# A two-layer transformer on one core: the first GELU rewritten with Tanh, and 63 softmax tiles given to VectorE

## The chip, the core and the metric

The kernel runs on one core of one Trainium2 chip. The metric is the device time in microseconds (us) of one execution, lower being better. A kernel's figure is the median of its timed runs, which were all taken in the fast state of the chip, unless said otherwise. PE is the tensor engine (PEld its weight loads), ACT the scalar engine, DVE the vector engine (VectorE), POOL GpSimd, SP the engine that starts most transfers.

## The reference, cut to what matters

Two layers, each an attention block and then a mixer with an MLP. S = 2048 rows, D = 448 columns, 16 heads of 28 columns, MLP width 1792, all in bf16.

```python
def _gelu(x):
    return jax.nn.gelu(x, approximate=True)

def _A_ref(x, wqkv, wo):                       # attention
    ...
    scores = jnp.einsum("bhqd,bhkd->bhqk", q, k) * (Dh ** -0.5)
    p = _softmax(scores, axis=-1)
    o = jnp.einsum("bhqk,bhkd->bhqd", p, v)
    ...
def _B_ref(x, w1, w2, w3, w4):                 # mixer and MLP
    h = _gelu(_layernorm(x, axis=-1) @ w1)     # the first GELU: 448 columns
    ...                                        # four groups of h shifted by -1, 1, -2, 2 rows
    x1 = x + hs                                # hs = shifted h @ w2
    h2 = _gelu(_layernorm(x1, axis=-1) @ w3) @ w4   # the second GELU: 1792 columns
    return x1 + h2

x = x + _A_ref(_layernorm(x, axis=-1), A_wqkv, A_wo)          # layer 0
x = x + _B_ref(_layernorm(x, axis=-1), B_w1, B_w2, B_w3, B_w4)
x = x + _A_ref(_layernorm(x, axis=-1), A_wqkv, A_wo)          # layer 1
x = x + _B_ref(_layernorm(x, axis=-1), B_w1, B_w2, B_w3, B_w4)
```

The softmax is the bulk of the element-wise work: 2 layers x 16 heads x 2048 x 2048 exponentials.

## The kernel before: the parts that matter here

**A fixed order per engine.** The kernel is written as Python generators. A list scheduler runs them once, when the kernel is built, with an assumed duration for every operation (the second argument of `op`) and a priority for every task, lower numbers first. What comes out is one fixed list of instructions for each engine. Each engine is given its list in that order, and semaphores hold an instruction back until its inputs are there. So the order comes from the assumed times, and the waits from the real ones: an engine whose next instruction isn't ready stands still, although a later one may be ready (PE does so at 610 us in the trace below).

**The exp stream.** `t_scores` makes bursts of three or two score tiles (128 keys x 512 queries each) in PSUM banks 0 to 2 or 3 and 4. One ACT instruction exponentiates the burst, 1536 or 1024 columns, into `PT`. `t_pv` then multiplies with the values. An exp waits for two things: its scores, and the PV matmuls that read its `PT` slots six bursts ago.

```python
def t_exp():
    for u, un in enumerate(units):               # un: the tiles of burst u
        yield ("wait", ("st", u))                # its scores
        if u >= 6:
            for (si, kb, j) in units[u - 6]:
                yield ("wait", ("pv", si, kb))   # PV of the burst whose PT slots it takes over
        ...
        yield op("act", 0.07 + n * w * 0.000833, lambda e, ...: e.activation(out=PT[:, s0:s0 + n, 0:w],
                 in_=ps[:, bk[0]:bk[0] + n, 0:w], func=ACT.Exp, scale=SCALE), ...)
```

**The mixers** run beside the exps of other rows. Their matmuls share PSUM banks 6 and 7 with the projections, and nearly all those banks are emptied by DVE. The GELUs are batched, because exp and `Gelu_apprx_tanh` don't share a table on ACT: the trace has a table load of 1283 ns before a batch and one before the next exp:

```python
# t_mixA, the first GELU: four groups of 112 features are evicted by DVE, then one GELU over all of them
ev = op("dve", c_ps(NW), lambda e, ...: e.tensor_copy(out=hT[0:112, grp, c0:c0 + NW], in_=ps[0:112, bi(b), 0:NW]), ...)
...
yield op("act", c_act(4 * NW), lambda e: e.activation(out=hT[0:112, :, c0:c0 + NW],
         in_=hT[0:112, :, c0:c0 + NW], func=ACT.Gelu_apprx_tanh), ..., tab="gelu")
```

**Fill matmuls.** `keep_pe_busy` puts matmuls without use (`wq_pad`, `ident`) where the plan sees PE idle, to keep its clock up. They go into free PSUM banks, and stand in PE's list like any other instruction.

**Dormant code.** A routine that exponentiates a score tile on DVE (`d_first`, `d_chain`) is there already, but `DVE_TILES` returns 0.

Of the kernel before, what the change touches and what calls it, by code (L numbers as in the profile page):

```python
# [7 lines left out]
ALU = mybir.AluOpType  # L8
# [448 lines left out]

def DVE_TILES(L, ch, g, p):
    return 0


PVB = 2
# [16 lines left out]
DPRIO = 3  # L479

def build_kernel(nc, A_x, A_wqkv, A_wo, B_x, B_w1, B_w2, B_w3, B_w4, out, n_layers=2):
# [13 lines left out]
    KSL = 6  # L495
# [4 lines left out]
    FS = 65536.0  # L500
    E0, E1, E2, E3 = 0.99992525, 0.69583285, 0.22606939, 0.07802301
# [43 lines left out]
    def n_dve(si):  # L545
        L, ch, g, p, kts, first, last = segs[si]
        if CHUNKS[L][ch][1] < 4:
            return 0
        return DVE_TILES(L, ch, g, len(kts))

    seg_kb = []
    seg_d = []
    stream = []
    dlist = []
    for si_, (L_, ch_, g_, p_, kts_, fi_, la_) in enumerate(segs):
        n_ = CHUNKS[L_][ch_][1]
        per = 4 // n_
        nd = n_dve(si_)
        kbs = [tuple(kts_[i:i + per]) for i in range(0, len(kts_), per)]
        dk = list(range(len(kbs) - nd, len(kbs)))  # L560
        seg_kb.append(kbs)
        seg_d.append(dk)
        for kb in range(len(kbs)):
            for j in range(4):
                if kb in dk:
                    dlist.append((si_, kb, j))
                else:
                    stream.append((si_, kb, j))
    units = []
    pos = 0  # L570
    while pos < len(stream):
        n_ = 3 if len(units) % 2 == 0 else 2
        units.append(stream[pos:pos + n_])
        pos += n_
    units_in = {}
    for u_, un_ in enumerate(units):
        units_in.setdefault(un_[-1][0], []).append(u_)
    slot_of = {}
    unit_of = {}
    for u_, un_ in enumerate(units):  # L580
        for k_, b_ in enumerate(un_):
            slot_of[b_] = 5 * ((u_ // 2) % 3) + (0 if u_ % 2 == 0 else 3) + k_
            unit_of[b_] = u_
# [4 lines left out]
    with st:  # L588
# [36 lines left out]
        kT = sb("kT", [128, 4, 512 * KSL], BF16)  # L625
        qT = sb("qT", [128, 4, 1024], BF16)
        vaug = sb("vaug", [128, 4 * KSL, 512], BF16)
# [14 lines left out]
        qd = sb("qd", [128, 512], FP32)  # L642
        ub = sb("ub", [128, 3, 512], FP32)
        rb = sb("rb", [128, 512], FP32)
# [18 lines left out]
        UB = ["u0", "u1", "u2"]  # L663
        xst = h2T[:, :, :].rearrange("p a b -> p (a b)").rearrange("p (t d) -> p t d", d=D)
# [28 lines left out]
        def vslot(L, t):  # L693
            return t if L == 0 else (t + 17 if t < 7 else t - 7)
# [418 lines left out]
        def t_fct(L, p, pp):  # L1113
            for g in range(4):
                yield ("wait", ("bc", L, p, g))
                yield ("wait", ("bc", L, pp, g))
            yield op("dve", 0.2, lambda e: e.tensor_tensor(out=dbc[:, L, p, :], in0=bcb[:, L, p, :], in1=bcb[:, L, pp, :], op=ALU.subtract),
                     reads=[("bcb", L, p, g) for g in range(4)] + [("bcb", L, pp, g) for g in range(4)], writes=[("dbc", L, p)])
            yield op("dve", 0.2, lambda e: e.tensor_scalar(out=db29[:, L, p, :], in0=dbc[:, L, p, :], scalar1=M29, scalar2=None, op0=ALU.mult),
                     reads=[("dbc", L, p), (("cols",), 1)], writes=[("db29", L, p)])  # L1120
            yield ("sig", ("db29", L, p))
            yield op("act", 0.25, lambda e: e.activation(out=fct[:, L, p, :], in_=dbc[:, L, p, :], func=ACT.Exp, scale=SCALE),
                     reads=[("dbc", L, p)], writes=[("fct", L, p)], tab="exp")
            yield ("sig", ("fct", L, p))

# [38 lines left out]
        def t_qp(si):  # L1164
            L, ch, g, p, kts, first, last = segs[si]
            yield ("wait", ("db29", L, p[1]))
# [3 lines left out]
                     reads=[qk, ("db29", L, p[1])], writes=[qk])  # L1170
            yield ("sig", ("qp", si))

        def unit_banks(u):
            return (0, 1, 2)[:len(units[u])] if u % 2 == 0 else (3, 4)[:len(units[u])]

# [11 lines left out]
        def d_chain(blk, ys, pd):  # L1187
            si, kb, j = blk
            w, s = num1(ys), slot_of[blk]
# [3 lines left out]
            q = qd[:, :]  # L1193
            pdt = PD[:, s, :]
            yield ("acq", ["q"])
            yield op("dve", c_ps(512), lambda e: e.scalar_tensor_tensor(out=q, in0=lo, scalar=E2 / E3 * FS, in1=lo, op0=ALU.add, op1=ALU.mult),
                     reads=[("yd", w)], writes=[("qd",)])
            yield op("dve", c_ps(512), lambda e: e.scalar_tensor_tensor(out=q, in0=q, scalar=E1 / E3 * FS * FS, in1=lo, op0=ALU.add, op1=ALU.mult),
                     reads=[("yd", w), ("qd",)], writes=[("qd",)])
            yield op("dve", 0.45, lambda e: e.tensor_scalar(out=pdt, in0=q, scalar1=E3 / FS ** 3, scalar2=E0, op0=ALU.mult, op1=ALU.add),  # L1200
                     reads=[("qd",)], writes=[("pd", s)])
            yield ("rel", "q")
# [3 lines left out]
            yield ("sig", ("db", si, kb, j))  # L1206

        def d_late(blk):
            pd = yield ("acq", PDS)
            slot_of[blk] = int(pd[2:])  # L1210
            ys = yield ("acq", YS)
            b = yield ("acq", MISC[0:2])
            yield from score_ops([blk], [bi(b)])
            late.discard(blk)
            yield ("spawn", d_first(blk, b, ys, pd), 1)

        late = set()

        def t_scores():
# [6 lines left out]
            pend = []  # L1226
            for u, un in enumerate(units):
# [5 lines left out]
                for blk in un:  # L1233
                    si = blk[0]
                    if si != cur:
                        for d_ in pend:
                            late.add(d_)
                            yield ("spawn", d_late(d_), 1)
                        cur = si
                        pend = [(si, kb, j) for kb in seg_d[si] for j in range(4)]  # L1240
                        total = len(pend)
                        yield ("sig", ("segstart", si))
                    yield from seg_ready(si, seg_kb[si][blk[1]])
                blks, banks = list(un), [b_ for b_ in unit_banks(u)]
                extra = []
                if pend and not late:
                    us = units_in[cur]
                    quota = -(-total * (us.index(u) + 1) // len(us))
                    for d_ in list(pend):
                        L = segs[cur][0]  # L1250
                        if len(blks) >= 4 or total - len(pend) >= quota:
                            break
                        if d_[2] in [b_[2] for b_ in blks] or any(("k", L, segs[cur][2], kc_of(L, kt)) not in SC.events for kt in seg_kb[cur][d_[1]]):
                            continue
# [3 lines left out]
                        slot_of[d_] = int(got[2][2:])  # L1258
                        pend.remove(d_)
                        blks.append(d_)  # L1260
                        banks.append(bi(got[0]))
                        extra.append((d_, got))
                yield from score_ops(blks, banks)
                for d_, got in extra:
                    yield ("spawn", d_first(d_, *got), 1)
                yield ("sig", ("st", u))
            for d_ in pend:
                yield ("spawn", d_late(d_), 1)

        def t_exp():  # L1270
            for u, un in enumerate(units):
                yield ("wait", ("st", u))
                if u >= 6:
                    for (si, kb, j) in units[u - 6]:
                        yield ("wait", ("pv", si, kb))
                bk = unit_banks(u)
                s0 = slot_of[un[0]]
# [7 lines left out]
                for (si, kb, j) in un:  # L1285
                    if j == 3:
                        yield ("sig", ("kb", si, kb))
# [5 lines left out]
        def t_pv():  # L1293
            yield ("wait", ("start",))
            yield ("acq", ["b5"])
            for si in range(len(segs)):
# [3 lines left out]
                todo = [kb for kb in range(len(kbs)) if kb not in seg_d[si]]  # L1300
                dtodo = list(seg_d[si])
# [4 lines left out]
                while todo or dtodo:  # L1306
                    if dtodo and (not todo or all(("db", si, dtodo[0], j) in SC.events for j in range(4))):
                        batch = [dtodo.pop(0)]
                        for j in range(4):
                            yield ("wait", ("db", si, batch[0], j))  # L1310
                        buf, key = PD, "pd"
                    else:
                        batch = todo[:PVB]
                        del todo[:PVB]
                        for kb in batch:
                            yield ("wait", ("kb", si, kb))
                        buf, key = PT, "pt"
                    for kb in batch:
                        for kt in kbs[kb]:
                            yield ("wait", ("v", L, kt))  # L1320
                    yield ("ready", [(key, slot_of[(si, kb, j)]) for kb in batch for j in range(4)] + ([("psw", 5)] if done == 0 else []))
                    for kb in batch:
                        for i, kt in enumerate(kbs[kb]):
                            vs = vslot(L, kt)
                            for j in range(4):
                                s = slot_of[(si, kb, j)]
# [4 lines left out]
                        if buf is PD:  # L1331
                            for j in range(4):
                                yield ("rel", "pd%d" % slot_of[(si, kb, j)])
# [21 lines left out]
        def t_norm(si):  # L1355
# [25 lines left out]
            if (L, ch) != (1, len(CHUNKS[1]) - 1):  # L1381
                yield ("acq", ["rT"])
# [5 lines left out]
                yield ("acq", ["rb"])  # L1388
# [395 lines left out]
```

## Time and profile before

| | before |
|---|---|
| median of 4 timed runs (range) | 1135.35 us (1133.80 to 1138.58) |
| ACT, PE, DVE, POOL busy in its first profile | 92, 94, 41, 22% |
| exp instructions, table loads | 819, 32 |

The first profile fell in the slow state: its first part and its clock row (tenths of full speed in 40 slices) are

```profile
span 1164.7 us, 34325 instructions
PE 1091.5 (94%) x15669; PEld 427.6 (37%) x15669; DVE 481.9 (41%) x946; ACT 1068.3 (92%) x922; POOL 258.0 (22%) x453
PEclk9888888888888888878888888888888888888888
```

The granted clock (the share of full speed at which PE was allowed to run) was 0.850 on the mean. For comparisons I use a second profile of the same kernel, run e1 below: 1130.14 us, clock 0.995. Its page, first part, chain of waits, and two groups of the costliest instructions (busy us, mean ns of one, then the engine's idle time before them and what ended it):

```profile
PE 1021.3 (91%) x15666; PEld 415.0 (37%) x15669; DVE 483.8 (43%) x946; ACT 1057.2 (94%) x922; POOL 257.7 (23%) x453
...
ACT 69%; PE 21%; DMA 3%; DVE 3%; POOL 1%; issue 1%; SPq 0%; ACTq 0%; POOLq 0%; DVEq 0%
...
L1280 ACT ACTIVATE PT<-ps 128x1536 bf16<-128x1536 f32 (+1 forms) x819 | 934.4, 1331 | 12.3 <-PE ps L1147 10.5
...
L1688 PE MATMUL ps<-wq_pad,ident 128*32 128x256 bf16 x3892 | 174.8, 275 | 3.2 <-DVE qT L1034 1.3
```

At full clock ACT is 69% of the chain that ended last. Its exps take 934 us and wait only 12 us in all. PE is 91% busy, but 175 us of that are fills. The table of stretches, from a second profile of the same kernel (columns: stretch, length, then busy us of PE, PEld, DVE, ACT and POOL, the clock, and the share and rate of DMA):

```profile
232.00:406.00 174.00, 158.00 (x2421) 63.07 (x2417) 60.94 (x104) 169.30 (x140) 35.32 (x60) 0.98 0.16 33
580.00:754.00 174.00, 159.72 (x2350) 64.88 (x2343) 80.37 (x175) 173.38 (x150) 29.15 (x59) 1.00 0.23 69
1080.00:1128.00 48.00, 43.37 (x826) 28.21 (x818) 17.88 (x35) 17.00 (x36) 9.49 (x21) 1.00 0.07 22
```

In the middle (232 to 928 us) ACT is busy for 97 to 99.6% of the time and DVE for 35 to 46%. In the last 48 us, nearly all of it the tail after the last exp (which ends at 1081.4 us), PE works and ACT is mostly idle. The kernel is bound by ACT and then by a tail of mixer work. These groups of ACT instructions, kept apart by shape (from a second profile of the same kernel; busy us, mean ns of one, then the engine's idle time before them and what ended it), are what the change goes for:

```profile
L1280 ACT ACTIVATE PT<-ps 128x1536 bf16<-128x1536 f32 x410 | 632.2, 1542 | 9.6 <-PE ps L1147 8.0
L1280 ACT ACTIVATE PT<-ps 128x1024 bf16<-128x1024 f32 x409 | 458.1, 1120 | 2.7 <-PE ps L1147 2.5
...
L1280 ACT ACT_TABLE_LOAD x15 | 19.2, 1283 | 0.3
L1526 ACT ACTIVATE hT<-hT 112x2048 bf16<-112x2048 bf16 x7 | 13.4, 1913 | 0.1
L1526 ACT ACT_TABLE_LOAD x8 | 10.3, 1283 | 0.1
```

### The profile page before, as it was taken

To read this page: it belongs to the slowest core of one execution; us is meant where nothing else is said; L and a number is where in the kernel's file an instruction comes from. 1 tells how busy PE (TensorE), PEld (TensorE's weight loads), DVE (VectorE), ACT (ScalarE), POOL (GpSimd) and SP (SyncE) were. 2 spreads that over 40 slices of the span, in tenths; PEclk is the share of its full clock that TensorE was granted. 3 is DMA by queue.
4 is the path that set the end of the run, shared out by engine and by line. 5 is a ranking of instruction groups with operands and counts; after the bars stand their busy time and mean duration, and the time that the engine had idled before them with its cause. 6 is when DMAs were issued, how large, how long until landed. Compare 5 with 4: busy or idle time off the path is not lost.

```text
span 1164.7 us, 34325 instructions
## 1 busy us (share of the span) xinstructions
PE 1091.5 (94%) x15669; PEld 427.6 (37%) x15669; DVE 481.9 (41%) x946; ACT 1068.3 (92%) x922; POOL 258.0 (22%) x453
## 2 busy tenths in 40 slices
PE   5999999999998989899999999999999999999898
PEld 2333333343333333223333433343333333344464
DVE  7763214422434334542466334513453523454332
ACT  5968999999999999989999999999999999999942
POOL 3221213302333013420243001102351300231121
PEclk9888888888888888878888888888888888888888
DMA  3483112003021022210311022313211110220100
GB/s 105 122 214 104 39 53 48 15 11 94 17 42 30 12 70 52 42 24 20 85 42 36 26 88 76 119 57 107 66 34 29 30 47 12 50 53 16 15 14 22
DMA packets 94666, 62.21 MB, mean 53 GB/s; under 512 B 64568, under 2 KB 84344, under 8 KB 94520
## 3 DMA queue, kind: packets, MB, share of 16 engines
q1 hardware_dynamic: 91256, 55.53, 18.3%
q0 software_dynamic: 2304, 3.67, 1.3%
q8 instruction: 123, 2.02, 0.8%
q10 hardware_dynamic: 960, 0.80, 0.2%
q14 instruction: 23, 0.19, 0.0%
HBM read 27.12 MB, written 15.71 MB: 37 GB/s over the span
## 4 chain that ended last, share of the span: by engine, by line
PE 49%; ACT 42%; DMA 4%; DVE 3%; POOL 1%; SPq 1%; issue 1%; ACTq 0%; DVEq 0%
ACT PT L1280 35%; PE ps L709 27%; PE ps L1147 12%; PE ps L700 10%; ACT h2T L1648 4%; DMA ub<-uscr 1%; ACT hT L1526 1%; ACT L1280 1%; ACT L1526 1%; ACT L1648 1%; DMA rT<-ub 1%; DVE xn L853 1%; PE ps L1688 1%; DMA xT<-xn 1%; DMA PT<-in_A_wqkv_dram 0%
## 5 line engine op out<-in xcount | busy, mean ns | idle before, releaser
L1280 ACT ACTIVATE PT<-ps 128x1536 bf16<-128x1536 f32 (+1 forms) x819 | 945.5, 1285 | 32.9 <-PE ps L1147 29.5
L1147 PE MATMUL ps<-qT,kT 32*128 32x512 bf16 (+1 forms) x2304 | 325.6, 367 | 28.7 <-ACT PT L1280 21.3
L700 PE MATMUL ps<-PT,vaug 128*32 128x512 bf16 (+1 forms) x2304 | 271.0, 381 | 0.2 <-DVE ub L1371 0.2
L1147 PEld LDWEIGHTS ps<-qT,kT 32*128 32x128 bf16 x2304 | 80.0, 91 | 343.6 <-ACT PT L1280 224.0
L1688 PE MATMUL ps<-wq_pad,ident 128*32 128x256 bf16 x3892 | 191.0, 292 | 2.3 <-DVE qT L1034 1.3
L709 PE MATMUL ps<-xT,w 128*32 128x512 bf16 (+1 forms) x2240 | 188.2, 388 | 3.4 <-DMA xT<-xn 2.2
L709 PE MATMUL ps<-w,h2T 128*32 128x448 bf16 x1624 | 121.3, 389 | 13.1 <-ACT h2T L1648 13.1
L1688 PEld LDWEIGHTS ps<-wq_pad,ident 128*32 128x32 bf16 x3892 | 112.9, 100 | 43.0 <-issue 18.1
L1639 DVE CAST h2T<-ps 128x512 bf16<-128x512 f32 (+2 forms) x112 | 67.7, 605 | 118.7 <-PE ps L709 110.5
L700 PEld LDWEIGHTS ps<-PT,vaug 128*32 128x32 bf16 x2304 | 71.5, 95 | 101.1 <-issue 86.8
L1393 POOL TENSOR_TENSOR otn<-ub,rb 128x512 bf16<-128x512 f32 (+1 forms) x32 | 38.6, 1206 | 289.4 <-DMA rb<-rscr 283.5
L709 PEld LDWEIGHTS ps<-xT,w 128*32 128x32 bf16 x2240 | 62.4, 98 | 63.6 <-issue 34.1
L709 PEld LDWEIGHTS ps<-w,h2T 128*32 128x32 bf16 x1624 | 44.9, 101 | 56.1 <-issue 17.7
L961 POOL TENSOR_TENSOR sq<-kT 128x512 bf16<-128x512 bf16 (+2 forms) x32 | 30.1, 941 | 118.5 <-DVE kT L975 118.4
L709 PE MATMUL ps<-xT,wk_pad 128*32 128x512 bf16 (+2 forms) x576 | 49.9, 392 | 0.9 <-DVE xT L876 0.6
L961 POOL TENSOR_TENSOR sq<-qT 128x512 bf16<-128x512 bf16 x28 | 29.3, 1048 | 95.3 <-DVE qT L1008 85.9
L709 PE MATMUL ps<-xT,wq_pad 128*32 128x512 bf16 x512 | 47.7, 417 | 0.7 <-DVE vaug L1050 0.5
L1371 DVE SCALAR_TENSOR_TENSOR ub<-ub,fct,ps 128x512 f32<-128x512 f32 x24 | 17.9, 747 | 69.6 <-PE ps L700 67.2
L1384 DVE RECIPROCAL rT<-rT 16x128 f32<-16x128 f32 (+1 forms) x32 | 30.0, 936 | 38.4 <-DMA rT<-ub 38.4
L709 PE MATMUL ps<-wv,xT 128*32 128x448 bf16 x512 | 43.6, 381 | 1.1 <-DVE vaug L1050 0.8
L1660 DVE TENSOR_TENSOR x_res<-x_res,ps 128x448 f32<-128x448 f32 x16 | 9.9, 621 | 83.1 <-PE ps L709 83.1
L709 PE MATMUL ps<-wo_pad,otn 128*32 128x448 bf16 x512 | 42.2, 384 | 2.1 <-DVE x_res L1444 2.1
(133 smaller groups left out, 892.9 us busy)
## 6 DMA issues: line engine op xcount, KB each, us to landing
rb<-rscr SPq DMA_DIRECT2D x28, 256.0 KB
uscr<-ub SPq DMA_DIRECT2D x24, 256.0 KB
ub<-uscr SPq DMA_DIRECT2D x24, 256.0 KB
xnd<-xn SPq DMA_DIRECT2D x28, 128.0 KB, 1.8
x_res<-in_A_x_dram POOLq DMA_DIRECT2D x16, 224.0 KB, 2.9
xd<-x_res SPq DMA_DIRECT2D x16, 224.0 KB, 1.9
x_res<-xd SPq DMA_DIRECT2D x16, 224.0 KB
out_dram<-obf SPq DMA_DIRECT2D x16, 112.0 KB
```

The source lines that it names most:

```text
L700: return lambda e: e.matmul(out=out, lhsT=lhsT, rhs=rhs, start=start, stop=stop, **kw)
L709: r.append(e.matmul(out=out[c:c + w, :], lhsT=lhsT[:, c:c + w], rhs=rhs, start=start, stop=stop, tile_position=(0, c)))
L961: return op("pool", 0.15 + NW * 0.0018, lambda e: e.tensor_tensor(out=sq[:, si, 0:NW], in0=src, in1=src, op=ALU.mult), reads=rk, writes=[( ...
L1147: yield op("pe", max(0.055, 0.22 / nc_ * NW / 512.0), lambda e, i=i, kc=kc, j=j, g=g, a=a, NW=NW, bank=bank: e.matmul(out=ps[:, bank, i * ...
L1280: yield op("act", 0.07 + n * w * 0.000833, lambda e, bk=bk, s0=s0, n=n, w=w: e.activation(out=PT[:, s0:s0 + n, 0:w], in_=ps[:, bk[0]:bk[0] ...
L1371: yield op("dve", c_ps(NW), lambda e: e.scalar_tensor_tensor(out=u, in0=u, scalar=fct[:, L, p[1], g:g + 1], in1=ps[:, 5, 0:NW], op0=ALU.mu ...
L1384: yield op("dve", 0.75, lambda e: e.reciprocal(out=rT[0:4 * n, :], in_=rT[0:4 * n, :]), reads=[("rT",)], writes=[("rT",)])
L1393: yield op("pool", 0.2 + NW * 0.0021, lambda e: e.tensor_tensor(out=otn[:, g, 0:NW], in0=u, in1=rb[:, 0:NW], op=ALU.mult), reads=[uk, ("rb ...
L1526: yield op("act", c_act(4 * NW), lambda e: e.activation(out=hT[0:112, :, c0:c0 + NW], in_=hT[0:112, :, c0:c0 + NW], func=ACT.Gelu_apprx_tanh),
L1639: ev = op("dve", c_ps(NW), lambda e, fch=fch, b=b: e.tensor_copy(out=hb[:, fch, 0:NW], in_=ps[:, bi(b), 0:NW]), reads=[("ps", bi(b))], wri ...
L1648: yield op("act", c_act(nl * NW), lambda e: e.activation(out=h2T[:, 0:nl, 0:NW], in_=h2T[:, 0:nl, 0:NW], func=ACT.Gelu_apprx_tanh), reads= ...
L1688: return [e.matmul(out=ps[32 * c:32 * c + 32, bi(b), 0:256], lhsT=ident[:, 32 * c:32 * c + 32], rhs=wq_pad[:, 0, 0:256], start=True, stop= ...
```

## The change

The intent is to take work from ACT, the bound, and give it to DVE, which is idle more than half of the time.

1. **Tanh GELU.** The first GELU is written out with Tanh, which needs no table change beside exp: DVE evicts z = 0.5x, POOL squares, DVE, ACT Tanh, DVE. Eight batched GELUs become 32 short Tanh, and 16 table loads go.
2. **Tiles on DVE.** In chunks 0 to 3 of layer 0 and 0 to 2 of layer 1, some 6% of a segment's score tiles (3% in one chunk), 63 in all, are taken as an extra head of a score burst. A tile goes to bank 6 or 7, if a bank, a `yd` and a `PD` buffer are free in the plan. Five DVE operations make the exp. The chain of the last four has priority 5, behind nearly everything else.
3. **Plumbing.** Bursts are put together on the fly; three shared `fb` buffers serve the chain, the Tanh and the normalization; there is one KV slot less; bias differences are made per group of heads; a few more normalizations go through PE.

```diff
+DPRIO = 5
+DLO = 4
+DHI = 8
+def DRATE(L,ch,g): return {(0,0):.06,(0,1):.06,(0,2):.06,(0,3):.03,(1,0):.06,(1,1):.06,(1,2):.06}.get((L,ch),0)
 ...
 # t_scores
+                    for kb in range(kb0 + DLO, min(kb0 + DHI, nkb)):
+                        ...
+                        got = yield ("try", [MISC[0:2], YS, PDS])
+                        if got is None:
+                            break
+                        blk = (si, kb, js[0])
+                        home[blk] = ("pd", int(got[2][2:]))
 ...
 # d_chain, after d_first (yd <- scaled scores) has emptied the bank
-            yield ("acq", ["q"])
+            fr = yield ("acq", FB, [("yd", w)])
             yield op("dve", c_ps(512), ... q = (lo + c) * lo ...)
             yield op("dve", c_ps(512), ... q = (q + c) * lo ...)
-            yield op("dve", 0.45, lambda e: e.tensor_scalar(out=pdt, in0=q, ...))
+            yield op(DTS[0], DTS[1], lambda e: e.tensor_scalar(out=pdt, in0=q, ...))
             yield op("dve", c_ps(512), ... PD = hi * 128 + PD, as int16 ...)
 ...
 # t_mixA
-                    ev = op("dve", c_ps(NW), ... tensor_copy ...)
+                    ev = op("dve", c_ps(NW), ... tensor_scalar, times 0.5 ...)
+                    yield ("spawn", t_tanh(L, t0, grp, hT[0:112, grp, c0:c0 + NW], NW, hk), pr)
-                yield op("act", ... Gelu_apprx_tanh over the four groups ...)
+        def t_tanh(L, t0, grp, z, NW, hk):
+            yield op("pool", 0.2 + NW * 0.0021, ... f = z * z ...)
+            yield op("dve", 0.1 + NW * 0.00108, ... f = (f + 0.25 / GK) * z ...)
+            yield op("act", c_act(NW), ... f = Tanh(scale * f) ..., tab="exp")
+            yield op("dve", 0.1 + NW * 0.00108, ... z = (f + 1) * z ...)
```

Counted in the built programs: exps 819 to 794, table loads 32 to 16, DVE instructions 946 to 1355, fill matmuls 3892 to 3092.

## The prediction

> **What bounds it now.** The page's first part: ACT busy 1068 of 1165 us (92%), PE 1092 (94%), DVE 482 (41%), POOL 258 (22%). In the stretches table ACT is 54 to 58 us busy in nearly every 58 us between 116 and 1102 us. PE's 94% is inflated: 3892 fill matmuls (line 1688) run 191 us, most between 58 and 232 and between 754 and 928 us; in 406 to 580 and 928 to 1102 they take only 16 to 17 of 174 us, so there PE is nearly full too. The chain of waits agrees: PE 49%, ACT 42%. From 1112 us on (after the last exp) it is PE alone, about 52 us. So: ACT bounds the light stretches, ACT and PE together the mixer stretches, PE the tail.
>
> **What ACT loses** (instruction counts from the two built programs):
> - 63 score tiles leave: 794 exp instructions for 819. A pair of 1536 and 1024 columns costs 2.27 us in the timeline (48 in 54.41 us), so about 0.43 us a tile plus 25 fixed parts: 28 us.
> - The mixer's first GELU (8 batches, 14.4 us) becomes 32 Tanh (28 of 512, 4 of 256 columns), about 15 us: no gain by itself. But table loads go from 32 to 16. The Trainium skill (ScalarE: Activation LUTs, "Table sets: the hidden batching unit") puts tanh in exp's set; the built program has no load before a Tanh. A load is 1.283 us in this trace: 20 us.
> Together about 47 us of ACT.
>
> **What it adds.** DVE: five operations for each of 63 tiles, estimated 0.5 to 0.75 us each from like operations (TENSOR_SCALAR from PSUM 0.745, SCALAR_TENSOR_TENSOR 0.747): about 210 us; two more per Tanh: about 43 us. DVE goes to about 720 us, some 65%. Where POOL runs too, one TENSOR_SCALAR from SBUF took 965 ns instead of 499, so more is possible. POOL gains 32 squares, about 32 us. The fourth head rides in a score burst: 25 fewer bursts on PE; fills drop from 3892 to 3092. The three layer-1 g=3 normalizations and one more go through PE instead of DMAs: small.
>
> **How much is critical.** The tiles lie in chunks 0 to 3 of layer 0 and 0 to 2 of layer 1, over half where PE still runs fills, so most of the saving there counts. At the end it does not: in the new program six 512-column GELU tiles of the chunk before last, and its second half of work, come after the last exp; before they came ahead of it. The tail grows by an estimated 12 to 18 us of PE work. I expect about 30 of 47 us.
>
> **Time:** 1105 us, 8 in 10 between 1084 and 1128. Chances: faster by over 2% 0.70, within 2% 0.27, slower 0.03.
>
> **What the profile will show if right.**
> 1. ACT busy about 1020 us, with 16 table loads and 794 exps.
> 2. DVE about 720 us, chain operations 0.5 to 0.8 us each.
> 3. Stretch 58 to 232 us of before shortened most; ACT's share of the middle stays above 94%.
> 4. Time from last exp to end grows from 52 to about 65 us.
> 5. Fill time on PE down by about 40 us; PE's share of the chain up.
> 6. Waits of scores for ACT fall; no large wait of PE on DVE `PD`.
>
> **What would make it wrong.** DVE in order: five-operation chains delay PSUM evictions, PE waits for banks 6 and 7 and the scores stall (then waits of PE on DVE grow by tens of us, near 1125). DVE operations slowed by POOL beyond 1 us each. The other way, PE may have more slack in the unprofiled runs (1135 against 1165 us profiled, where the granted clock is 0.85) and the whole 47 us appear: about 1088.

## The result, and the profile after

| | before | after |
|---|---|---|
| median of 4 timed runs (range) | 1135.35 us (1133.80 to 1138.58) | 1120.95 us (1118.73 to 1121.54) |
| mean granted clock of 32 fast runs of before, 4 of after | 0.990 | 0.976 |

The ratio is 0.9866, with a 95% interval of 0.9840 to 0.9891. Every ratio here is the mean time of one kernel's fast runs over that of the other's in the same rounds, so it is not quite the ratio of the medians. The change won 14 us where I had expected 30. The time lies in the range; "faster by over 2%", the likeliest class, did not happen.

The page after, with the lines that answer to those of before:

```profile
PE 1009.0 (90%) x14936; PEld 405.6 (36%) x14939; DVE 721.7 (65%) x1355; ACT 1010.1 (90%) x910; POOL 305.9 (27%) x481
...
ACT 58%; PE 26%; DVE 10%; DMA 3%; POOL 2%; issue 1%; SPq 0%; ACTq 0%; DVEq 0%
...
L1286 ACT ACTIVATE PT<-ps 128x1536 bf16<-128x1536 f32 (+1 forms) x794 | 912.0, 1323 | 52.6 <-PE ps L686 28.6
...
L1699 PE MATMUL ps<-wq_pad,ident 128*32 128x256 bf16 x3092 | 140.9, 278 | 5.7 <-DVE x1b L1597 3.1
```

ACT's busy time fell by 1057.2 - 1010.1 = 47.1 us. But the idle time before exps went from 12.3 to 52.6 us, and DVE's share of the chain from 3 to 10%. The stretches of the middle show it too; ACT is no longer busy nearly all the time, and DVE's work in the first one has doubled. The last line is the tail:

```profile
232.00:406.00 174.00, 156.57 (x2296) 59.24 (x2294) 122.98 (x208) 163.79 (x138) 45.91 (x66) 0.97 0.15 34
580.00:754.00 174.00, 157.76 (x2317) 62.99 (x2316) 103.75 (x220) 164.61 (x145) 28.06 (x40) 0.98 0.21 67
1055.00:1117.00 62.00, 56.71 (x1074) 35.13 (x1066) 20.13 (x39) 23.46 (x42) 9.34 (x21) 1.00 0.06 19
```

ACT's groups after: 32 Tanh with no table load at their line, and 7 loads at the exps instead of 15.

```profile
L1540 ACT ACTIVATE fb<-fb 112x512 f32<-112x512 f32 x28 | 18.6, 669 | 0.0
...
L1286 ACT ACT_TABLE_LOAD x7 | 9.0, 1283 | 0.1
...
L1540 ACT ACTIVATE fb<-fb 112x256 f32<-112x256 f32 x4 | 2.7, 670 | 0.0
```

The Trainium skill says that tanh is in exp's table set (ScalarE: Activation LUTs, "Table sets: the hidden batching unit"); the trace agrees, with 16 loads left for the second GELU and the start. The chain's five operations on DVE:

```profile
L1201 DVE SCALAR_TENSOR_TENSOR PD<-yd,PD 128x512 int16<-128x512 int16 x63 | 49.2, 788 | 0.7
L1196 DVE SCALAR_TENSOR_TENSOR fb<-fb,yd 128x512 f32<-128x512 f32 x63 | 44.7, 719 | 0.5
L1194 DVE SCALAR_TENSOR_TENSOR fb<-yd 128x512 f32<-128x512 uint16 x63 | 43.9, 710 | 0.4
L1180 DVE TENSOR_SCALAR yd<-ps 128x512 int32<-128x512 f32 x63 | 43.1, 686 | 48.0 <-PE ps L1139 47.6
L1198 DVE TENSOR_SCALAR PD<-fb 128x512 bf16<-128x512 f32 x63 | 33.0, 532 | 0.4
```

The work of a tile is 0.69 + 0.71 + 0.72 + 0.53 + 0.79 = 3.43 us. But from the start of the first to the end of the last operation a tile took 7.7 us on the median and 24.3 at most.

**Where the time went.** Here is an account of both profiles (e1 for before), one execution each. "Idle" is the sum of all gaps of ACT that end between 60 us and the end of the last exp. The differences were taken before rounding.

| us | before (e1) | after | difference |
|---|---|---|---|
| start to first exp | 25.4 | 24.3 | -1.2 |
| ACT's idle | 22.2 | 52.0 | +29.8 |
| the rest up to the last exp, mostly ACT work | 1033.7 | 980.1 | -53.6 |
| tail after the last exp | 47.0 | 60.6 | +13.5 |
| span | 1128.4 | 1116.9 | -11.5 |

The work ahead of the last exp fell by more than 47 us because the last large batch of the second GELU moved behind the last exp: ACT works 22.1 us in the tail of after, 15.6 in that of before, 6.5 more. (No table load moved with it; there is one in the tail before and after.) So up to the last exp 53.6 + 1.2 = 54.8 us went, and 29.8 us of new idle time came back; the tail took 13.5 more.

The waits of ACT (what waited for what, total us, times, longest) name the new idle time. Before, then after:

```profile
ACT PT L1280 <- PE ps L1147: 10.5, 12, 2.7
ACT fct L1122 <- DVE dbc L1117: 10.2, 2, 7.1
```

```profile
ACT PT L1286 <- PE ps L686: 28.6, 12, 4.5
ACT PT L1286 <- PE ps L1139: 22.2, 26, 4.2
```

Before, exps waited 10.5 us, for scores only (L1147), and never for PV. After, they waited 28.6 us for PV (L686), which is new, and 22.2 us for scores (L1139). The 10.2 us for `fct`, a wait for bias differences, went with the plumbing; run e4 below, which has the plumbing alone, doesn't show it either.

The longest of the new gaps can be followed. ACT's timeline (start, length, instruction, idle before and its releaser), and the chain that ended last, in order of time:

```profile
611.75 1.45 ACT L1286 ACTIVATE PT<-ps 128x1536 bf16<-128x1536 f32 x1 [4.49 <-PE ps L686]
```

```profile
603.26 1.07 DVE xn L839 x2
604.33 0.60 DVE x1b L1597
...
607.13 1.32 DVE xn L839
608.45 0.54 DVE st L824
...
609.11 0.39 DVE PD L1198
609.51 0.60 DVE x1b L1597
...
610.13 0.63 DVE st L824
610.76 0.83 DVE xn L839
...
611.68 0.58 DVE PD L1201
...
612.31 0.34 PE ps L686
```

For nine microseconds the chain runs through DVE alone, apart from two short POOL operations that are cut out here. Mixer work (`xn`, `x1b`, `st`) and a tile's chain (`PD`) take turns there. PE's timeline shows two ways in which DVE's delay stops PE:

```profile
610.15 0.95 PE L1699 MATMUL ps<-wq_pad,ident 128*32 128x256 bf16 x28 [1.25 <-DVE x1b L1597]
...
612.31 0.39 PE L686 MATMUL ps<-PD,vaug 128*32 128x512 bf16 x1 [0.42 <-DVE PD L1201]
```

First, PE's next instruction is a fill into a bank that DVE hasn't emptied yet (`x1b`), and the PV behind it in PE's list, at 611.34, releases the exp. A fill is not free here: after the wait, PE works through 28 of them for 0.95 us ahead of that PV. Then a PV waits for the tile itself. Over the whole run these two kinds of instruction waited for the chain's last operation (us in total, times):

```profile
  PEld ps L686: 11.1, 12
  PE ps L686: 6.5, 7
```

A weight load and its matmul often wait for the same thing, so the two must not be added: PE's matmuls lost 6.5 us this way. Of the 12 waits of exps for PV, two (3.2 and 2.3 us) follow such a wait. Most of the others follow evictions on DVE, as above, or come while PE runs at half clock (see e11). All waits of PE's matmuls for DVE between 60 us and the last exp grew from 8.8 us before to 20.3.

### The profile page after: what moved, and what is told of

It is laid out like the page before. It is cut to its first block, busy times and chain, and to the rows that moved or that the text cites. A ratio compares the mean times of both kernels' runs of the same rounds, so it can differ in the third digit from the quotient of the medians.

```text
span 1116.9 us, 33256 instructions
## 1 busy us (share of the span) xinstructions
PE 1009.0 (90%) x14936; PEld 405.6 (36%) x14939; DVE 721.7 (65%) x1355; ACT 1010.1 (90%) x910; POOL 305.9 (27%) x481
## 4 chain that ended last, share of the span: by engine, by line
ACT 58%; PE 26%; DVE 10%; DMA 3%; POOL 2%; issue 1%; SPq 0%; ACTq 0%; DVEq 0%
ACT PT L1286 52%; PE ps L695 14%; PE ps L1139 6%; PE ps L686 5%; ACT h2T L1659 4%; DVE xn L839 2%; DMA ub<-uscr 1%; ACT fb L1540 1%; ACT L1659 1%; DVE qT L994 1%; DVE PD L1201 1%; DVE x1b L1597 1%; DVE PD L1198 1%; DVE st L824 1%; PE ps L1699 1%
## 5 line engine op out<-in xcount | busy, mean ns | idle before, releaser
L1286 ACT ACTIVATE PT<-ps 128x1536 bf16<-128x1536 f32 (+1 forms) x794 | 912.0, 1323 | 52.6 <-PE ps L686 28.6
L1139 PE MATMUL ps<-qT,kT 32*128 32x512 bf16 (+1 forms) x2304 | 315.4, 365 | 47.6 <-ACT PT L1286 37.6
L686 PE MATMUL ps<-PT,vaug 128*32 128x512 bf16 (+1 forms) x2241 | 246.9, 366 | 1.9 <-DVE ub L1367 1.1
L1139 PEld LDWEIGHTS ps<-qT,kT 32*128 32x128 bf16 x2304 | 78.2, 91 | 328.5 <-ACT PT L1286 286.1
L695 PE MATMUL ps<-xT,w 128*32 128x512 bf16 (+2 forms) x2240 | 169.0, 364 | 4.8 <-DMA xT<-xn 1.9
L1699 PE MATMUL ps<-wq_pad,ident 128*32 128x256 bf16 x3092 | 140.9, 278 | 5.7 <-DVE x1b L1597 3.1
L686 PEld LDWEIGHTS ps<-PT,vaug 128*32 128x32 bf16 x2241 | 68.0, 95 | 92.7 <-issue 76.0
L1699 PEld LDWEIGHTS ps<-wq_pad,ident 128*32 128x32 bf16 x3092 | 85.6, 97 | 36.4 <-issue 14.6
L1391 POOL TENSOR_TENSOR otn<-ub,fb 128x512 bf16<-128x512 f32 (+1 forms) x28 | 36.2, 1293 | 166.2 <-DMA fb<-rscr 159.0
L1180 DVE TENSOR_SCALAR yd<-ps 128x512 int32<-128x512 f32 x63 | 43.1, 686 | 48.0 <-PE ps L1139 47.6
L1538 POOL TENSOR_TENSOR fb<-hT 112x512 f32<-112x512 bf16 (+1 forms) x32 | 36.3, 1136 | 69.3 <-DVE hT L1520 66.3
L1201 DVE SCALAR_TENSOR_TENSOR PD<-yd,PD 128x512 int16<-128x512 int16 x63 | 49.2, 788 | 0.7
L1196 DVE SCALAR_TENSOR_TENSOR fb<-fb,yd 128x512 f32<-128x512 f32 x63 | 44.7, 719 | 0.5
L1194 DVE SCALAR_TENSOR_TENSOR fb<-yd 128x512 f32<-128x512 uint16 x63 | 43.9, 710 | 0.4
```

Source lines behind the costliest of these rows:

```text
L686: return lambda e: e.matmul(out=out, lhsT=lhsT, rhs=rhs, start=start, stop=stop, **kw)
L695: r.append(e.matmul(out=out[c:c + w, :], lhsT=lhsT[:, c:c + w], rhs=rhs, start=start, stop=stop, tile_position=(0, c)))
L1139: yield op("pe", max(0.055, 0.22 / nc_ * NW / 512.0), lambda e, i=i, kc=kc, j=j, g=g, a=a, NW=NW, bank=bank: e.matmul(out=ps[:, bank, i * ...
L1180: yield op("dve", c_ps(512), lambda e: e.tensor_scalar(out=y, in0=ps[:, bi(bank), :], scalar1=SCALE * L2E * FS, scalar2=-126.0 * FS, op0=A ...
L1194: yield op("dve", c_ps(512), lambda e: e.scalar_tensor_tensor(out=q, in0=lo, scalar=E2 / E3 * FS, in1=lo, op0=ALU.add, op1=ALU.mult), read ...
L1196: yield op("dve", c_ps(512), lambda e: e.scalar_tensor_tensor(out=q, in0=q, scalar=E1 / E3 * FS * FS, in1=lo, op0=ALU.add, op1=ALU.mult), ...
```

## The experiments

Each run's edit is against the kernel after, except for e1. All gave correct results. The times are medians of four timed runs (six for e12) with their ranges.

### e1: before, looked at once more

No edit: the kernel before, one look, to have its profile at full clock.

> The kernel before once more, for a profile in the fast state: the one at hand was taken at a granted clock of 0.85 and took 1165 us, the changed kernel's at 0.977, so the two cannot be set side by side. All theories: about 1134 us, ACT busy again 1068 us (its clock is not what was throttled). Theory DVE-delay (the chains on VectorE arrive late, PE waits for them in program order and the exponentials wait for PE): the fast profile of before shows under 15 us of ACT gaps over 0.7 us in the middle, against about 42 us in the changed kernel's. Rival tail theory (the saving is real in the middle and lost after the last exp): ACT gaps in the middle about alike in both, and the time after the last exp longer by 12 us or more in the changed kernel (61 us there).

It took 1130.14 us at clock 0.995. ACT was busy 1057 us and not 1068. Its gaps over 0.7 us add up to 17.2 us, somewhat over the 15 expected (10.2 of them are the waits for `fct`), against 43.6 in after; and the tail is 13.5 us shorter than after's. So there is something in both theories. Its profile is the one used above. The PE half of the chain in the first profile (PE 49%, ACT 42%) was the slow state's: here it is ACT 69%, PE 21%.

### e2, e3, e4: one part alone, and neither

```diff
# e2: no tiles, Tanh kept
-def DRATE(L,ch,g): return {(0,0):.06,(0,1):.06,(0,2):.06,(0,3):.03,(1,0):.06,(1,1):.06,(1,2):.06}.get((L,ch),0)
+def DRATE(L,ch,g): return 0
# e3: the batched GELU back, tiles kept
-   ev = op("dve", ... tensor_scalar, times 0.5 ...);  t_tanh(...) for each group
+   ev = op("dve", ... tensor_copy ...);  one op("act", ... Gelu_apprx_tanh ...) for the four groups
# e4: both edits, so that only the plumbing is left
```

> The changed kernel without its tiles on VectorE (rate 0; all else kept: 16 table loads, 819 exps, 0 tiles). DVE-delay theory: the Tanh alone keeps its 20 us of table loads and the tiles gave about nothing, so this is 1113 to 1123 us, equal to the changed kernel within 0.5%. Tail theory: the tiles' 28 us are lost only in part; this is 1128 us or more.

> The changed kernel with the batched GELU of before, tiles kept (34 loads, 793 exps, 65 tiles). DVE-delay theory: tiles alone give little, 1128 to 1138 us. Tail theory, and any in which the tiles' saving counts: 1112 to 1125 us.

> The changed kernel with neither tiles nor Tanh: what is left is the plumbing (one key slot fewer, normalization of some groups through PE, bias differences by group). All theories: 1130 to 1140 us, as before. If it is faster than before by over 0.5%, a part of the gain is the plumbing's.

| run | time (range) | ratio to before (95%) | idle of ACT | tail |
|---|---|---|---|---|
| e2, Tanh alone | 1122.68 (1114.19 to 1126.85) | 0.9887 (0.9836 to 0.9939) | 28.6 | 61.4 |
| e3, tiles alone | 1115.99 (1113.73 to 1116.86) | 0.9833 (0.9799 to 0.9867) | 34.0 | 50.7 |
| e4, neither | 1134.03 (1129.14 to 1138.86) | 0.9997 (0.9954 to 1.0039) | 18.5 | 47.6 |
| after, both | 1120.95 (1118.73 to 1121.54) | 0.9866 (0.9840 to 0.9891) | 52.0 | 60.6 |

The plumbing alone is worth nothing. The tiles alone win 1.7% and Tanh alone 1.1%; together they win 1.3% and not 2.8%. So what is lost is lost between the two. The expectation that tiles alone give little was missed: e3 came out at 1116 us and not at 1128 or more. The profiles, one execution each, show where the loss lies: the longer tail comes with Tanh, and the new idle time is more with both (52.0 - 22.2 = 29.8 us) than the two alone add up to (6.4 and 11.8). Why the Tanh version ends with more mixer work behind the last exp is not settled; e6 below rules one reason out.

### e5: is the plan wrong because its prices are too low?

Theory: the scheduler takes the chain for shorter than it is, so its order doesn't fit the chip. The edit gives it measured durations.

```diff
-DTS = ("dve", 0.45)
+DTS = ("dve", 0.53)
-   yield op("dve", c_ps(512), ...)          # the chain's three other operations
+   yield op("dve", 0.71, ...)   ... 0.72 ...   ... 0.79 ...
-   yield op("dve", 0.1 + NW * 0.00108, ...) # the two of the Tanh
+   yield op("dve", 0.2 + NW * 0.00108, ...)
    # likewise reciprocal 0.75 -> 0.93, xn of the second mixer half 0.53 -> 0.98
```

> The same arithmetic as the changed kernel; only the durations that its scheduler assumes for VectorE are set to what the traces measured (chain 0.71, 0.72, 0.53, 0.79 us for 0.68, 0.68, 0.45, 0.68; Tanh steps 0.75 for 0.65; reciprocal 0.93 for 0.75; one normalization 0.98 for 0.53). 66 tiles, 792 exps, 16 loads. The ledger so far: against before in the fast state the changed kernel has 54 us less ACT work ahead of the last exp, but 30 us more ACT gaps and 14 us more after the last exp. Plan theory (PE's order was laid out for a VectorE quicker than the real one, so PE reaches its waits early): gaps over 0.7 us fall from 44 us to 25 or less, 1100 to 1112 us. Load theory (VectorE is simply too full): gaps stay over 35 us, 1116 to 1125 us.

It took 1136.60 us (1132.84 to 1138.01), ratio 1.0009 (0.9976 to 1.0043): as slow as before the change. Idle of ACT was 70.6 us, with two gaps of 10.4 and 16.5 us, and one tile's chain took 30.8 us. That is above both expectations. The theory that wrong prices are the cause got no support: a better-informed plan of nearly the same load (66 tiles for 63) came out worse. It is one new order, though, and not a test of prices alone.

### e6: does the Tanh's own length make the tail?

Theory: Tanh needs more steps one after the other, so the last mixers end later. The edit gives chunks 2 and 3 of layer 1 the old batched GELU.

```diff
+            old = not direct and (L, tiles[0]) in ((1, 8), (1, 12))
     ...
+                    if old:   # tensor_copy eviction, then one batched Gelu_apprx_tanh, as before
```

> The changed kernel with the old batched GELU in the last two chunks of layer 1 that have the Tanh; 20 loads, 63 tiles, the program the same until about nine tenths of its exps. Theory that the longer Tanh path delays the last mixers and so makes the tail: time after the last exp falls from 61 to about 50 us, total 1108 to 1114 us. Theory that the tail is long because the exps end earlier while the mixer's PE work does not (its place in the order moves by one GELU tile only): tail 57 us or more, total 1116 to 1124 us.

It took 1126.45 us (1123.01 to 1131.14), ratio 0.9927 (0.9890 to 0.9964), and the tail was 61.7 us in its profile, no shorter than after's 60.6. The theory fell for these two chunks.

### e7: is it POOL getting in DVE's way, or DVE's load?

DVE operations are slower while POOL works. In after's trace the second mixer half's `xn` took 1016 ns with POOL busy (30 of them) and 503 without (2), and the chain's last operation 995 ns (22 of them) against 677 (41), while the chain's first, which reads PSUM, took 683 and 687. The Trainium skill has this (GPSIMD Engine Reference, "1. Specifications"): the SBUF interfaces are shared with VectorE, with contention for DVE instructions in a two-port mode or with two SBUF inputs. The rival is that DVE has too much to do. Moving the 32 squares of the Tanh from POOL to DVE lowers the contention and raises the load.

```diff
-            yield op("pool", 0.2 + NW * 0.0021, lambda e: e.tensor_tensor(out=f, in0=z, in1=z, op=ALU.mult), ...)
+            yield op("dve", 0.13 + NW * 0.00108, lambda e: e.tensor_tensor(out=f, in0=z, in1=z, op=ALU.mult), ...)
```

> The Tanh's squares on VectorE instead of POOL (32 operations, about 22 us more VectorE, 36 us less POOL), 65 tiles. Contention theory (VectorE's SBUF operations are stretched while POOL runs a tensor operation; in the trace the chain's last operation takes 995 ns with POOL busy and 677 without): chain operations shorten by 5% or more, gaps fall to 30 us or less, 1106 to 1115 us. Load theory: gaps grow, 1120 us or more.

It took 1146.06 us (1144.03 to 1148.95), ratio 1.0099 (1.0072 to 1.0126): slower than before the change. DVE went from 721.7 to 744.9 us busy, idle of ACT from 52.0 to 80.2 us. 23 us more of DVE work cost 25 us (1146.06 - 1120.95). Load fits. Contention was hardly lowered by this edit: the chain's five operations took 3.39 us a tile in sum, after 3.43, where the theory asked for 5% less. So the run doesn't show that contention costs nothing.

### e8: half of the tiles

If DVE's load is the cause, fewer tiles should lose less than they save.

```diff
-def DRATE(L,ch,g): return {(0,0):.06,(0,1):.06,(0,2):.06,(0,3):.03,(1,0):.06,(1,1):.06,(1,2):.06}.get((L,ch),0)
+def DRATE(L,ch,g): return {(0,0):.03,(0,1):.03,(0,2):.03,(0,3):.015,(1,0):.03,(1,1):.03,(1,2):.03}.get((L,ch),0)
```

> The changed kernel with half the rates: 39 tiles, 803 exps. Tiles-give-nothing-beside-Tanh theory: between no tiles (1122.7) and all (1121.0), so 1117 to 1125. Theory of too many tiles (an optimum between): 1105 to 1115 us, gaps 30 us or less.

With 39 tiles and 804 exps (the plan's count of 803 is one short) it took **1107.07 us** (1101.28 to 1116.57), ratio 0.9762 (0.9696 to 0.9827). This is the best version: its interval lies below after's, although it isn't settled whether it beats before by more than 2%. In its profile (1112.55 us, clock 0.982) DVE is busy 649.8 us, the idle of ACT 37.5 us against 52.0, waits of exps for PV fell from 28.6 to 4.3 us, and the tail is about the same, 60.0. Gaps over 0.7 us were 31.6 us, just above the 30 expected. So with 24 tiles less it gave back about 9 us of saved ACT work and got 14.5 us of idle time back. One gap alone makes up over a third of what is left; ACT's and PE's timelines:

```profile
714.98 3.71 ACT L1286 ACTIVATE PT<-ps 128x1536 bf16<-128x1536 f32 x3 [13.64 <-PE ps L1139]
```

```profile
709.03 0.62 PE L695 MATMUL ps<-xT,wk_pad 128*32 128x256 bf16 x16 [1.44 <-DMA xT<-xnd]
...
714.54 0.60 PE L1139 MATMUL ps<-qT,kT 32*128 32x512 bf16 x5 [0.79 <-DVE qT L1161]
```

The scores need the keys of layer 1's last rows. Their projection starts at 709.03, when the transposed rows of layer 0's last mixer have come in. The exp stream reached this point early and had to wait for the mixers: part of the lead wasn't kept at the layer boundary. This is a second limit, and it does not go with the number of tiles: the projection starts at 711.2 us in after, 710.6 in e2 (no tiles), 709.0 here and 713.6 and 711.8 in e10 and e12. By the time at which the same PV matmul ends, e8 was 33 us ahead of before at before's 721 us, and 16 at its 751; after was 17 and 14 ahead. So most of what half the tiles had won over after was lost again here.

### e9: the same tiles, chain first

If the place in DVE's queue is the cause, a high priority should cure it.

```diff
-DPRIO = 5
+DPRIO = 0.5
```

> The changed kernel with the VectorE chains at priority 0.5 in place of 5: 63 tiles, 794 exps, 16 loads as there; only the order on the engines differs. In the changed kernel a chain has 3.4 us of work but takes 7.7 us (median) and up to 24 us from its first operation to its last, because mixer and projection work is placed between; a PV that needs the tile then stops PE, and the exps behind it. Starvation theory: chain median under 5 us, ACT's waits for PV fall from 28.6 us to under 10, gaps over 0.7 us from 44 to 25 or less, 1100 to 1112 us. Load theory (VectorE is full, whoever goes first makes the other late): the waits move to evictions (scores and projections), gaps stay over 35 us, 1116 us or more.

It took 1135.61 us (1133.72 to 1136.81), ratio 1.0012 (0.9989 to 1.0035). The chains did become short, 3.3 us on the median against 7.7, and 6.4 at most, and exps waited less for PV. But they waited longer for scores:

```profile
ACT PT L1286 <- PE ps L1139: 44.0, 21, 20.8
...
ACT PT L1286 <- PE ps L686: 13.9, 10, 2.5
```

The longest wait, 20.8 us at 528 us, is for layer 1's first queries, which come from layer 0's mixers. In this order the mixers ran later: the first batch of the second GELU starts at 323.9 us, in after at 252.7. That they stood behind the chains on DVE is not shown; in the 30 us ahead of the wait no chain operation ran there. By the same PV matmul, the exp stream was 39 us ahead of before at before's 558 us and 4 at its 570. ACT's idle is 60.3 us, 8.3 more than after's, and the tail 70.7, 10.1 more, so that over half of what e9 lost against after lies behind the last exp, for a reason not looked into. So with another order of DVE's work others waited; the waits weren't removed.

### e10: half of the tiles, and priority 1

> Half the rates and the chains at priority 1: 36 tiles, 804 exps. Starvation theory: as good as or better than half the rates alone (1107.1), 1098 to 1108 us. Load theory: 1105 to 1115 us, no better than half alone.

```diff
-DPRIO = 5
+DPRIO = 1
     # and e8's DRATE
```

36 tiles, 805 exps: 1111.34 us (1105.72 to 1113.21), ratio 0.9794 (0.9753 to 0.9834), idle of ACT 32.2 us. It overlaps e8. Two different orders with about half of the tiles both beat the full number, which speaks against e8 being one lucky order, though it doesn't exclude it.

### e11: more fills, for the clock

The clock is lower after the change: 0.976 against 0.990. In the clock records of after's profile there are ten stretches at 0.5, 51.2 us in all, between 60 us and the last exp, in before's (e1) two, 10.2 us. Each is 3.413 us long or a multiple of it. The skill describes these (TensorE: Matmul & The Clock Gate, Part 1, "What's actually happening"): half rate after an idle window of about 3.4 us, with a window that runs freely, so that the number of slow matmuls varies by run. The trace agrees with the state and the length of the window; with the idle window only in part: in the 3.4 us ahead of eight of after's stretches PE was busy for 21 to 67%, but ahead of the two longest (13.7 and 10.2 us) for 85 and 98%. Rival theory: fewer fills (3892 to 3092), so a lower clock, so slower matmuls and late scores. The edit raises the target of the fills.

```diff
-    TARGET = 0.52
+    TARGET = 0.6
```

> The changed kernel with more fill matmuls (target 0.60 for 0.52: 3800 for 3092, as many as before had); the rest of its program in the same order. The changed kernel's PE ran 51 us at half clock before the last exp, against 10 us in before's fast profile. Clock theory (fewer fills let the clock drop, and the slow PE makes the gaps): half-clock time under 20 us, gaps over 0.7 us fall from 44 to 30 or less, 1105 to 1114 us. Theory that the stops come first and the clock only follows: half-clock time stays over 30 us or the gaps stay over 38 us, 1116 to 1124 us.

With 3800 fills and otherwise the same order it took 1116.71 us (1113.69 to 1123.20), ratio 0.9855 (0.9817 to 0.9892), within after's interval. The mean clock of its four runs was 0.9805, and its profiled run, the slowest, had 61 us at half clock. So the fills hardly raised the clock, and the question is open: over the 82 fast runs of before, after and e2 to e12 whose clock is on record, with each kernel's own mean taken off, time and clock go together at -8.16 us for +0.01 of clock (correlation -0.93). By that slope, about 11 of after's microseconds go with its lower clock, an estimate. The lower clock alone could make as much: 0.01 of 1117 us is 11 us of PE time. But waits can also make PE idle and so lower the clock, and the slope doesn't say which comes first. Of the 43.6 us of ACT's gaps over 0.7 us in after, 13.3 us lie inside half-clock stretches; the gap at 607 us shown above has none near it.

### e12: half of the tiles, and the late mixers earlier

To win the tail back, e8's tiles were combined with higher priorities for layer 1's mixers.

```diff
-    return {..., (1, 0): 3, (1, 1): 3, (1, 2): 2.5, (1, 3): 2, (1, 4): 1.6}[(L, ch)]
+    return {..., (1, 0): 3, (1, 1): 2, (1, 2): 1.6, (1, 3): 1.5, (1, 4): 1.4}[(L, ch)]
     # and e8's DRATE
```

> Half the rates (39 tiles, 803 exps, as e8) and the mixers of the last layer's chunks raised in the order (1,1): 2 for 3, (1,2): 1.6 for 2.5, (1,3): 1.5 for 2, (1,4): 1.4 for 1.6, so that the last big GELU batch stands before the last exps again, as in before; 18 loads. Theory that the 13.6 us of longer tail are a loss of their own: time after the last exp falls from 60.5 to about 50 us, gaps stay at 30 to 40, total 1095 to 1103 us. Theory that the end is set by PE and mixer work that has to be done anyhow, so what leaves the tail comes back ahead of the last exp: total 1104 to 1114 us, as half alone (1107.1).

It took 1120.96 us (1114.31 to 1124.76), ratio 0.9858 (0.9822 to 0.9893). That is slower than either theory expected. Against e8's profile the tail shrank from 60.0 to 49.4 us, as wanted, but ACT's idle grew from 37.5 to 49.1 and its work ahead of the last exp by 9 us. What left the tail came back in the middle.

## Why the prediction was right or wrong

1. **ACT's saving: right.** Expected "about 47 us of ACT", measured 47.1, with 794 exps and 16 loads. The 1020 us of point 1 came out as 1010, because I had subtracted from the slow profile's 1068 and not from 1057.
2. **DVE's cost: right.** 721.7 us for "about 720"; the five operations took 532 to 788 ns, in the range of 0.5 to 0.8.
3. **The middle: the numbers held, the reading didn't.** ACT's share of the stretches between 58 and 928 us was 94.1 to 94.6%, just "above 94%". But before it was over 97% from 232 us on, so that passing this mark already meant a loss. The mark was set too low to find it. The stretch up to 232 us did shorten most: by the same PV matmul, the lead over before grew from 9.5 to 16 us between before's 69 and 224 us, reached 21 at 489, and was back at 13.5 at 751.
4. **The tail: right.** Forecast to grow by 12 to 18 us, measured 13.5, and the six 512-column GELU tiles do stand behind the last exp.
5. **Fills: right.** 174.8 to 140.9 us is 34 less, for "about 40"; PE's share of the chain rose from 21 to 26%.
6. **"No large wait of PE on DVE PD": about right as it stands, but it looked past the loss.** PE's matmuls waited 6.5 us on `PD`. The exps waited 28.6 us on PV, where they hadn't waited before, and the list has no line for that. Scores' weight loads waited for ACT a little less, as expected (303.9 to 286.1 us).

The step that failed is "I expect about 30 of 47 us": my sum had a term for the tail, but none for new idle time of ACT in the middle. That term measured +29.8 us (22.2 to 52.0). The work ahead of the last exp fell more than I had counted, since 6.5 us of it moved into the tail, and so the sum is -53.6 - 1.2 + 29.8 + 13.5 = -11.5 us in the profiles, and -14 in the timed medians. What I had written under "What would make it wrong" is what happened, to a smaller degree: DVE in order delays the chains and the evictions, and PE's waits for DVE grew by 11.5 us, not by tens. I had given DVE's free half the value of free time. In a fixed order its delays reach the exps in two ways, through a tile's PV and through evictions that PE waits for. How much of the 29.8 us is DVE's and how much the clock's is not separated.

What the experiments show of the cause: neither the plan's prices (e5), nor the Tanh's own length in the last chunks (e6), nor the tiles' place in the queue (e9) is the cure; more DVE work cost about as much as it lasts (e7), and less DVE work went with shorter times (e8, e10). What they don't show: how much of each result is the luck of one order, since every edit makes the scheduler lay out a new one, how much of the loss the lower clock causes rather than follows, and whether the three `fb` buffers, which chain, Tanh and normalization share, hold them up (no run has more of them). Brought to the same clock of 0.99 by the slope above, an estimate, after would be at 1109 us and e8 at 1107, so that e8's gain over after goes mostly together with its higher clock. In e8 itself two runs at 0.997 took 1101 us and two at 0.98 took 1113 and 1117.

## What to carry to other kernels

An engine that is 43% busy isn't free by 57%: when engines work in a fixed order and the receiving one also empties the banks that the bound engine's inputs come through, cost the work that you move there as queueing on the critical path as well, and look at the gaps of the bound engine and not only at its busy time. Move half first: here about 39 tiles were better than 63, by 14 us as timed and by about 2 at the same clock, an estimate. Take the bound from a profile at the same clock as the timed runs, because the first one here named PE where it was ACT.

## What the Trainium skill lacked or had wrong

- ScalarE: Activation LUTs, "What ACT_TABLE_LOAD costs": with the drain it counts about 2.7 us for one change of tables. Here the load takes 1.28 us and the next instruction starts 0.02 us later, so that a change costs 1.3 us. ACT's timeline of after, around one GELU batch:

```profile
514.15 1.28 ACT L1659 ACT_TABLE_LOAD   x1
515.45 6.18 ACT L1659 ACTIVATE h2T<-h2T 128x7168 bf16<-128x7168 bf16 x1
521.64 1.28 ACT L1286 ACT_TABLE_LOAD   x1
```

- GPSIMD Engine Reference, "1. Specifications": it says that DVE and POOL contend, but gives no size in that section. Here `PD<-yd,PD` took 995 ns with POOL busy and 677 without, `xn<-x1b` 1016 and 503 (only 2 without); `yd<-ps`, which reads PSUM, wasn't stretched (683 and 687).
- TensorE: Matmul & The Clock Gate, Part 1, "What's actually happening": it has half rate come after an idle window. Here a kernel with PE 90% busy ran 51 us of 1117 at half clock before the last exp, in ten stretches, and the two longest, 24 us together, follow windows in which PE was 85 and 98% busy by the trace. The page's two states don't have the 0.850 that the slow profile of before was granted nearly throughout, with this program on one core, and its third, the limiter at 13/16 (Part 1, "Seeing it yourself"), is said to need three busy cores.
- No page that I used says how a mean granted clock goes with the time of a kernel bound by ACT: here -8.16 us for +0.01, over 82 fast runs (a correlation).
